# Expert chosen from 8 tiles instead of 16, its first rows gathered in the scatters' queue, and half of the first block's product moved into the last two attention rounds

## The chip, the cores and the metric

The kernel runs on one core of a Trainium2 chip. A core has five engines with a queue of instructions each: TensorE (matmuls and transposes, PE in the profile, its weight loads PEld), VectorE (DVE), ScalarE (ACT), GpSimd (POOL) and SyncE (SP, which here only issues transfers). Transfers run on 16 DMA engines. The metric is the device time of one execution in microseconds; the median of the runs counts.

## The reference

Three parts, one behind the other, on 3072 rows of 384 numbers:

```python
for t in range(S):                                   # 1: attention with a decaying state, 4 x 8 heads of 48
    cur = np.einsum('bhd,bhe->bhde', u[None] * kt, vt)
    y[:, :, t] = np.einsum('bhd,bhde->bhe', rt, state + cur)
    state = wt[:, :, :, None] * state + np.einsum('bhd,bhe->bhde', kt, vt)

logits = x @ w_gate + modality_bias[modality_id]     # 2: one of 8 experts for each row
e_idx = np.argmax(logits, axis=1)
h = np.maximum(x[mask] @ w1[e], 0.0)                 #    F = 1024
out[mask] = gate_w[mask, None] * (h @ w2[e])

h = np.maximum(np.maximum(x @ w1, x @ w2), x @ w3)   # 3: a network of width 768
return (h @ w_out)
```

## The kernel before

**Attention** runs in 24 rounds, one for each tile of 128 rows (L895 on, `for i in range(NTILE)`). The rounds overlap: round i computes the scans of tile i+2 (`scan_f`, L745, at its start, and `scan_r`, L761), the scores of tile i+1 (`scores`), and the output of tile i (`output`, TensorE, L805 and L811). VectorE turns the output into x one round later (`output_x`, L830), so output(22) is TensorE's work in round 22 and x(22) is VectorE's at the start of round 23; x(i) goes to DRAM (`xs`). In each round GpSimd masks the scores of tile i+1 (`am`, L781), makes the u-term of tile i+2 (L708, L709), and scales v by its sum (L718), which x needs. SP issues the loads of tile i+3 (`nat`, `vt`) and of tile i+5 (`tq`), a round or so before they are used; ScalarE checks the w columns of tile i+4 as they come (`flags`, L723).

**Routing** goes in batches of tiles, 8, 8, 3, 2 and 3. Behind a batch's last tile `route_batch` is put in a list, and `slot()`, which is called some six times a round, runs a few steps of it: about 16 small VectorE instructions, two small TensorE matmuls, and at the end one scatter for each tile (`scatter`, L297, an indirect transfer issued by GpSimd). A scatter writes the row numbers of a tile, sorted by expert, into a DRAM list (`order`). `do_scatters` issues them one at a time, at two places of a round.

**Choosing.** Behind the second batch (`NG` = 16 tiles) `choose_first` takes the expert that has the most rows so far (13 small VectorE instructions, and a flag `few` if it has fewer than 512). `first_load` loads that expert's weights in seven pieces (w1 three, w2 four). `settle` is a GpSimd memset of the places that the scatters have read, so it waits until they have landed; behind it `first_ids` gathers row numbers from `order`, and `first_rows` gathers the rows of the first two blocks from `xs`. `split_w1` and `split_w2` cut the weights into a high part (ScalarE's copy, `w1h`) and a low part (`w1l`, `w2l`, L500, VectorE or GpSimd), since each product is made of three matmuls in a reduced format.

**The first network** goes over 13 blocks of 256 rows: blocks 0 and 1 of the chosen expert, an extra block X with that expert's remaining rows, and ten more. `x_part` turns the gathered rows into columns (`xh`, `xl`: TensorE transposes, L1129); `g1` is the first product in four quarters of 18 matmuls, `g2` the second. The last batch's routing and the plan of the blocks (the generator `chain`, which `go(n)` runs n steps of) lie within block 0. **The second network** follows over six pairs of blocks.

What lies where around the end of attention is written out by hand: a table of hooks, {(round, place): functions}, the counts in `FIRST_GO` for `go`, and the counts of dummy matmuls in `WARM`. The code's order is each engine's order.

Of the kernel before, what the change touches and what calls it, by code (L numbers as in the profile page):

```python
# [33 lines left out]
W2_FIRST = range(8)  # L34
RATE = (2, 6, 4)
# [6 lines left out]
FIRST_GO = (2, 2, 4, 0, 0, 2, 4, 4, 0, 0, 6)  # L42
WARM = (16, 6, 4, 0, 3, 6, 6, 3, 3)
# [3 lines left out]
def kernel(ctx: ExitStack, tc: tile.TileContext, rkw_t, v_t, vrk, u, modality, w_gate, bias, w1, w2, v1, v2,  # L47
# [17 lines left out]

    TW = 256
    EARLY = 2
    NG = -(-E * TW // 128)

    batches = [(t, 8) for t in range(0, NG, 8)]  # L70
    for n in (3, 2, 3):
        batches.append((sum(batches[-1]), n))
    assert NG % 8 == 0 and sum(batches[-1]) == NTILE
# [12 lines left out]
    def mmt():  # L86
        return pools["mm"].tile([128, 512], F32, tag="mm", name="mm")
# [152 lines left out]

    scatters = []

    def route_batch(batch, then=(), lead=0):
# [20 lines left out]
        for _ in range(lead and GAP[0]):  # L264
            yield SLOT
# [34 lines left out]
        scatters.extend([lambda c=c: scatter(c) for c in range(nb)])  # L300

# [9 lines left out]
    def do_scatters(n=NTILE):  # L311
        if scatters and "filled" in carry:
            carry.pop("filled")()
        for sc in scatters[:n]:
            sc()
        carry["scattered"] = carry.get("scattered", 0) + len(scatters[:n])
        del scatters[:n]
# [275 lines left out]
    def attention(hooks):  # L593
        with ExitStack() as es:
# [242 lines left out]
            rate = [1]  # L837
# [21 lines left out]
            carry["warm"] = warm  # L859
            loads, rows = constants_rest(pes)  # L860
# [34 lines left out]
            for i in range(NTILE):  # L895
# [31 lines left out]
                if i < NTILE - 3:  # L927
                    do_scatters(1)
# [11 lines left out]
                slot()  # L940
                if i:
                    warm(WARM[5] if i == NTILE - 1 else WARM[6] if i == NTILE - 2 else WARM[4 if i % NC == NC - 1 else 3])
                    T[i - 1].clear()
                if i < NTILE - 3:
                    do_scatters(1)
# [3 lines left out]
                if i and i == t0 + nb:  # L949
                    later.append(route_batch((t0, nb), (choose_first,) if i == NG else (), LEAD))  # L950
                    rate[0] = RATE[(i == NG) + 2 * (i > NG)]
# [5 lines left out]
            while later:  # L957
                run(later.pop(0))
# [80 lines left out]
    class Experts:  # L1039
# [74 lines left out]
        def room(self, s, eng=POOL):  # L1114
            s["xin"] = [self.px.tile([128, DM], F32, tag="xin", name="xin") for _ in range(2)]
            for xin in s["xin"]:
                eng.memset(xin, 0.0)
# [173 lines left out]
    def first_rows(j):  # L1291
        for half in range(2):
            ex.gather(T[j], half, NG * 128)

    def first_x():
        for half in range(2):
            go(FIRST_GO[half])
            ex.x_part(T[0], half)
            carry["warm"](WARM[7 + half])
        go(FIRST_GO[2])  # L1300

# [30 lines left out]
    def first_block(vw):  # L1332
# [6 lines left out]
        for s, cur in enumerate(seq):  # L1339
            nx = seq[s + 1] if s <= N - 1 else None  # L1340
            for q in range(4):
                if s == 0:
                    ex.g1((q,), lambda: go(FIRST_GO[2 * q + 3]))
# [5 lines left out]
                elif s < EARLY:  # L1349
                    if s == 0:  # L1350
                        ex.split_w2((2 * q, 2 * q + 1), W2_FIRST)
                        go(FIRST_GO[2 * q + 4])
# [62 lines left out]
    def rest():  # L1415
# [3 lines left out]
        with tc.If(lastv > 0):  # L1419
# [7 lines left out]
            with ExitStack() as es:  # L1427
# [14 lines left out]
                with tc.If(fewv > 0):  # L1442
                    for j in range(1, EARLY):
# [9 lines left out]
    with tc.manual_schedule():  # L1453
# [4 lines left out]
        def ex_room(j, eng):  # L1458
            ex.room(T[j], eng)
        attention({(NG + 3, "mid"): [chosen, bind(first_load, 0, 0)],  # L1460
                   (NG + 3, "end"): [bind(first_load, 0, 1)],
                   (NG + 4, "mid"): [bind(first_load, 0, 2)],
                   (NG + 4, "end"): [bind(first_load, 1, 0)],
                   (NG + 5, "mid"): [bind(first_load, 1, 1)],
                   (NG + 5, "end"): [bind(first_load, 1, 2), bind(ex.open_rows, wes)],
# [71 lines left out]
```

## Time and profile before

| | |
|---|---|
| median of 3 runs | 784.94 us (784.89 to 790.58) |
| the profiled execution | 783.83 us, of which the span from first to last instruction is 781.7 |
| attention, routing | to about 222 us |
| first network | about 222 to 500 us |
| second network | to the end |
| busy shares of the span | PE 92%, PEld 83%, DVE 67%, POOL 46%, ACT 40% |

A row of the timeline gives start, duration, engine, line, operation, `out<-in`, the number of merged instructions, and in brackets the idle time of the engine before it with what ended it. The rows below all come from the profiled execution.

### The profile page before, as it was taken

What the parts mean: (1) busy time and instruction counts of PE and PEld (TensorE: products, weight loads), DVE (VectorE), ACT (ScalarE), POOL (GpSimd) and SP (SyncE); (2) the same over time, 40 slices, a digit from 0 to 9 for tenths busy, and PEclk for the clock granted to TensorE, in tenths of its full rate; (3) what the DMA queues carried; (4) which work ended last, traced back from release to release, by engine and by line L of the source; (5) the groups of instructions that cost most, each with busy time, mean ns of one, the idle gap of its engine ahead of it and who ended that gap; (6) DMA issues with size and microseconds to landing.
All of it is one profiled execution on the core that took longest, in us unless ns stands there. A gap on an engine that the chain in (4) does not pass through costs nothing.

```text
span 781.7 us, 13036 instructions
## 1 busy us (share of the span) xinstructions
PE 718.9 (92%) x4745; PEld 649.5 (83%) x4746; DVE 519.9 (67%) x975; ACT 313.9 (40%) x705; POOL 362.8 (46%) x389
## 2 busy tenths in 40 slices
PE   6889887887699999999999999999999999999991
PEld 3778787777589989999999998798988989889891
DVE  5999999999668798878897889624224243242320
ACT  5556545444241465566666653221212222112210
POOL 7698769858676477766665354120100201002000
PEclk9799989979789999999999999999999999999996
DMA  9878879968412322222226134020100200001000
GB/s 243 201 203 244 225 178 187 205 176 217 81 52 90 93 71 63 80 80 66 63 73 223 41 125 158 1 82 0 68 15 0 82 1 21 20 1 41 0 17 29
DMA packets 32382, 74.57 MB, mean 95 GB/s; under 512 B 5973, under 2 KB 19061, under 8 KB 32308
## 3 DMA queue, kind: packets, MB, share of 16 engines
q1 hardware_dynamic: 27508, 64.15, 30.5%
q0 software_dynamic: 4800, 9.49, 3.8%
q8 instruction: 39, 0.64, 0.4%
q14 instruction: 35, 0.29, 0.1%
HBM read 87.96 MB, written 14.38 MB: 131 GB/s over the span
## 4 chain that ended last, share of the span: by engine, by line
issue 39%; DVE 23%; PE 21%; POOL 7%; DMA 5%; ACT 1%; SPq 1%; POOLq 0%; DVEq 0%; ACTq 0%
PE mm L1142 7%; PE mm L1141 6%; PE mm L1140 6%; DVE prod L745 3%; DVE prod L761 3%; POOL out_dram L1225 3%; DMA tq<-in_rkw_t_dram 3%; DVE w1l L500 2%; POOL w2l L500 1%; DVE rt L754 1%; DVE tq L730 1%; DVE sh L714 1%; DVE x L830 1%; DMA w2r<-in_moe_w_dram 1%; DVE kvb L818 1%
## 5 line engine op out<-in xcount | busy, mean ns | idle before, releaser
L1205 DVE TENSOR_TENSOR w2r<-mm,w2r 128x512 f32<-128x512 f32 x72 | 49.7, 690 | 146.9 <-PE mm L1142 146.8
L1225 POOL DMA_INDIRECT out_dram<-w2r,oi_all x24 | 25.9, 1078 | 247.2 <-ACT w2r L1224 246.5
L1140 PE MATMUL mm<-w1h,vh 128*128 128x512 f32 x324 | 127.7, 394 | 1.3 <-DVE w2r L1205 1.3
L1142 PE MATMUL mm<-w1h,vl 128*128 128x512 f32 x324 | 127.1, 392 | 0.0
L1141 PE MATMUL mm<-w1l,vh 128*128 128x512 f32 x324 | 125.9, 389 | 0.0
L1142 PE MATMUL mm<-xh,w1l 128*128 128x256 f32 x312 | 89.4, 287 | 3.0 <-DVE w1l L500 3.0
L1142 PE MATMUL mm<-hh,w2l 128*128 128x256 f32 x312 | 89.1, 286 | 1.0 <-POOL w2l L500 0.8
L1141 PE MATMUL mm<-hl,w2h 128*128 128x256 f32 x312 | 88.5, 284 | 1.0 <-DVE hl L1154 1.0
L1140 PE MATMUL mm<-hh,w2h 128*128 128x256 f32 x312 | 89.2, 286 | 0.0
L1140 PE MATMUL mm<-xh,w1h 128*128 128x256 f32 x312 | 88.5, 284 | 0.0
L1141 PE MATMUL mm<-xl,w1h 128*128 128x256 f32 x312 | 88.3, 283 | 0.2 <-DVE xl L1134 0.2
L1207 ACT CAST w2h<-w2r 128x512 fp32r<-128x512 f32 x36 | 22.3, 621 | 136.7 <-DVE w2r L1205 136.6
L1140 PEld LDWEIGHTS mm<-w1h,vh 128*128 128x128 f32 x324 | 60.9, 188 | 14.0 <-DVE w2r L1205 2.0
L1142 PEld LDWEIGHTS mm<-w1h,vl 128*128 128x128 f32 x324 | 60.8, 188 | 14.0
L1141 PEld LDWEIGHTS mm<-w1l,vh 128*128 128x128 f32 x324 | 60.8, 188 | 13.3
L500 DVE TENSOR_TENSOR w1l<-w1r,w1h 128x512 fp32r<-128x512 f32 x66 | 51.6, 835 | 24.3 <-ACT w1h L498 24.2
L500 POOL TENSOR_TENSOR w2l<-w2r,w2h 128x384 fp32r<-128x384 f32 x40 | 46.2, 1160 | 40.2 <-ACT w2h L498 38.4
L805 PE MATMUL yb<-nat,am 128*128 128x56 f32 x384 | 53.0, 297 | 12.3 <-DVE lh L832 9.7
L1142 PEld LDWEIGHTS mm<-xh,w1l 128*128 128x128 f32 x312 | 59.8, 192 | 5.1 <-DVE w1l L500 5.1
L805 PEld LDWEIGHTS yb<-nat,am 128*128 128x128 f32 x384 | 50.7, 213 | 14.3 <-POOL am L781 5.3
L1142 PEld LDWEIGHTS mm<-hh,w2l 128*128 128x128 f32 x312 | 59.7, 191 | 2.6 <-POOL w2l L500 1.2
L1141 PEld LDWEIGHTS mm<-hl,w2h 128*128 128x128 f32 x312 | 59.7, 191 | 1.5 <-DVE hl L1154 1.4
(244 smaller groups left out, 1757.2 us busy)
## 6 DMA issues: line engine op xcount, KB each, us to landing
w1r<-in_moe_w_dram SPq DMA_DIRECT2D x10, 1536.0 KB, 7.1
w2r<-in_moe_w_dram SPq DMA_DIRECT2D x10, 1536.0 KB
nat<-in_vrk_dram SPq DMA_DIRECT2D x24, 608.0 KB, 6.9
tq<-in_rkw_t_dram SPq DMA_DIRECT2D x46, 288.0 KB, 6.8
stg<-in_moe_w_dram SPq DMA_DIRECT2D x18, 384.0 KB, 3.1
vt<-in_v_t_dram SPq DMA_DIRECT2D x24, 192.0 KB, 7.0
x2t<-raw SPq DMA_DIRECT2D x12, 384.0 KB, 2.4
w1r<-x2t SPq DMA_DIRECT2D x12, 384.0 KB, 3.8
```

Of the source, the lines that this page charges most:

```text
L500: eng.tensor_tensor(out=lo, in0=src, in1=hi.bitcast(F32), op=ALU.subtract)
L714: DVE.tensor_reduce(out=s["sh"], in_=heads(s["k"]), axis=AX.X, op=ALU.add)
L730: DVE.tensor_scalar(out=wr, in0=wr, scalar1=W_LO, scalar2=W_HI, op0=ALU.max, op1=ALU.min)
L745: DVE.tensor_tensor_scan(out=prod, data0=f[:, 1023:1535], data1=d1f, initial=0.0, op0=ALU.mult, op1=ALU.add)
L761: DVE.tensor_tensor_scan(out=prod[:, 0:511][:, ::-1], data0=f[:, 1025:1536][:, ::-1], data1=d1r[:, 0:511][:, ::-1], initial=0.0, op0=ALU.m ...
L805: PE.matmul(yb[:, h * DV:(h + 1) * DV], lhsT=s["am"][:, 4 * (h % 2) + h // 2, :], rhs=s["v"][:, h, :], start=(h == 0), stop=(first and h = ...
L1140: PE.matmul(oc, lhsT=wh[:, kk, sl], rhs=xh[:, kk, :], start=first and kk == 0, stop=False)
L1141: PE.matmul(oc, lhsT=wh[:, kk, sl], rhs=xl[:, kk, :], start=False, stop=False)
L1142: PE.matmul(oc, lhsT=wl[:, kk, sl], rhs=xh[:, kk, :], start=False, stop=last and kk == nk - 1)
L1205: DVE.tensor_tensor(out=hv, in0=o, in1=hv, op=ALU.max)
L1207: ACT.copy(self.h2h[:, c, :], hv)
L1225: ins = POOL.indirect_dma_start(out=out[:, :], out_offset=bass.IndirectOffsetOnAxis(ap=ids[q][:, 0:1], axis=0), in_=ob, in_offset=None, bo ...
```

## The change

- The batches become 8, 8, 5 and 3, and `NG` becomes 8: the expert is chosen from the first 8 tiles. Its weights are loaded in rounds 13 to 19, one piece a round, instead of rounds 19 to 22.
- `settle` and the eight gathers (four of ids, four of rows) go into the list of scatters, behind the first batch's eight and two empty entries; `do_scatters` issues them two a round like scatters. The row tiles are filled with zeros by ScalarE in round 14 instead of by GpSimd.
- Block 0's columns and the first three `split_w1` come in round 22 behind the scores, the first quarter of `g1` in round 23, the second quarter behind the last round, and the rest of the routing within it. Products during attention use the small pool `tp`.
- Four of the eight low parts of w2 are made by GpSimd instead of VectorE, two and two in round 23.
- The dummy matmuls of the last two rounds and those around block 0's columns are gone (6 + 6 + 3 + 3).

```diff
-W2_FIRST = range(8)
-RATE = (2, 6, 4)
+W2_FIRST = range(4, 8)
+RATE = 4
-FIRST_GO = (2, 2, 4, 0, 0, 2, 4, 4, 0, 0, 6)
-WARM = (16, 6, 4, 0, 3, 6, 6, 3, 3)
+FIRST_GO = (8, 1, 7, 2, 6)
+WARM = (16, 6, 4, 0, 3)
...
-    NG = -(-E * TW // 128)
...
+    batches = [(0, 8), (8, 8), (16, 5), (21, 3)]
+    NG = sum(batches[0])
...
+        if sum(batch) == NG and lead:
+            scatters.extend([lambda: None] * 2 + [lambda: settle(0, NG)] + first_gathers)
...
-                if i < NTILE - 3:
-                    do_scatters(1)
+                do_scatters(2 if i >= NTILE - 2 else 1)
...
-    def first_ids(j):
-        do_scatters(max(0, NG - carry["scattered"]))
-        if j == 0:
-            settle(0, NG)
-        for q in (2 * j, 2 * j + 1):
-            ex.gather_ids(oi_all[:, q, :], idxg[:, q:q + 1])
+    def first_ids(q):
+        ex.gather_ids(oi_all[:, q, :], idxg[:, q:q + 1])
+
+    def first_room():
+        ex.open_rows(wes)
+        for j in range(EARLY):
+            ex.room(T[j], carry["zero"])
...
+    def first_rows(q):
+        ex.gather(T[q // 2], q % 2, NG * 128)
+    first_gathers.extend([lambda q=q: first_ids(q) for q in range(2 * EARLY)])
+    first_gathers.extend([lambda q=q: first_rows(q) for q in range(2 * EARLY)])
...
-                   (e - 3, "uterm"): [bind(first_ids, 0)],
-                   (e - 2, "start"): [bind(ex.split_w1, (0, 1, 2))],
-                   (e - 2, "uterm"): [bind(ex_room, 0, POOL), bind(first_rows, 0)],
...
-                   (e - 2, "end"): [bind(first_ids, 1), bind(ex.split_w1, (3, 4, 5), "h")],
-                   (e - 1, "mid"): [bind(ex.split_w1, (3, 4, 5), "l"), bind(ex_room, 1, POOL), bind(first_rows, 1)],
...
-                   (e, "mid"): [first_x, bind(ex.split_w2, (0, 1), W2_FIRST, "h")],
+        hooks = {(13, "mid"): [chosen, bind(first_load, 0, 0)],
+                 (14, "end"): [first_room],
+                 (e - 2, "uterm"): [first_x, bind(ex.split_w1, (0, 1, 2))],
+                 (e - 2, "late"): [bind(ex.split_w1, (3, 4, 5), "h")],
+                 (e - 1, "uterm"): [bind(ex.split_w1, (3, 4, 5), "l"), bind(ex.g1, (0,)),
+                                    bind(ex.split_w2, (0, 1), W2_FIRST)],
+                 (e - 1, "mid"): [bind(ex.split_w2, (2, 3), W2_FIRST)],
+                 (e, "mid"): [bind(ex.g1, (1,), rest_of_routing)],
+                 (e, "end"): [bind(ex.split_w2, (4, 5), W2_FIRST)]}
+        for q in range(1, 7):
+            hooks[(13 + q, "mid")] = [bind(first_load, q // 3 if q < 6 else 1, q if q < 3 else q - 3)]
```

On GpSimd's queue in rounds 21 and 22 the kernel before has, in a row, three scatters, the memset of `settle`, two gathers of ids, and only then the scaling of v (`nat<-nat,sh`) and the masking of the scores (`am`):

```order
L708 TENSOR_TENSOR nat<-nat,u_b 128x384
L709 TENSOR_TENSOR nat<-nat 128x384
L297 DMA order<-idg,places 24576x2 x3
L309 MEMSET places 128x16
L1110 DMA oi_all<-order,idxg 128x2 x2
L718 TENSOR_TENSOR nat<-nat,sh 128x448
L781 AFFINE_SELECT am<-am 128x512 x2
L1117 MEMSET xin 128x384 x2
L1121 DMA xin<-xs,oi_all 128x384 x2
```

The kernel after has the memset and the gathers in rounds 16 to 20, one at a time (the first of them here; lines are three to seven further on):

```order
L721 TENSOR_TENSOR nat<-nat,sh 128x448
L784 AFFINE_SELECT am<-am 128x512 x2
L711 TENSOR_TENSOR nat<-nat,u_b 128x384
L712 TENSOR_TENSOR nat<-nat 128x384
L313 MEMSET places 128x8
L721 TENSOR_TENSOR nat<-nat,sh 128x448
L1117 DMA oi_all<-order,idxg 128x2
L784 AFFINE_SELECT am<-am 128x512 x2
L711 TENSOR_TENSOR nat<-nat,u_b 128x384
L712 TENSOR_TENSOR nat<-nat 128x384
L1117 DMA oi_all<-order,idxg 128x2
```

So the memset and all eight gathers leave the stretch in which L718 and `am` of the last tiles are made.

On TensorE the kernel after has, in rounds 22 and 23, the transposes of block 0's rows (`tp<-ident,xin`) between the scores and gate(23), and the first quarter of the product (`tp<-xh,w1h` and its two fellows, 18 rows, of which two stand here) behind output(22) and a routing matmul:

```order
L780 MATMUL mm<-rt,kt 128x128 x8
L1136 MATMUL tp<-ident,xin 128x128 x6
L705 MATMUL tp<-wgb,vt 128x64 x3
L808 MATMUL yb<-nat,am 128x56 x8
L814 MATMUL yb<-sbd_149,rt 128x112 x4
L269 LDWEIGHTS sut_bf
L269 MATMUL lgps<-oh,sut_bf 128x40
L270 LDWEIGHTS ones_bf
L270 MATMUL lgps<-ohx,ones_bf 128x40
L1147 MATMUL tp<-xh,w1h 128x256
L1148 MATMUL tp<-xl,w1h 128x256
```

Before, these transposes and the whole first product stand behind output(23), its routing matmul and dummies.

On SP's queue the kernel after has, in rounds 13 and 14, a piece of w1 between the loads of one round and those of the next; before, the first of these pieces stands behind the loads of round 19:

```order
L677 DMA tq_162<-in_rkw_t_dram 48x1536 x2
L1282 TENSOR_LOAD gctl
L1282 ISA x2
L1288 ISA
L1288 DMA w1r<-in_moe_w_dram 128x1024
L836 DMA xs<-x 128x384
L682 DMA nat<-in_vrk_dram 128x1216
L687 DMA vt<-in_v_t_dram 128x384
L677 DMA tq_163<-in_rkw_t_dram 48x1536 x2
L1288 ISA
L1288 DMA w1r<-in_moe_w_dram 128x1024
```

The queue itself is in order, so in rounds 13 to 19 a weight piece now goes out ahead of the next round's `nat`, `vt` and `tq`.

## Rows read from the trace of the kernel before

**Rows 1.** Stretches: busy us and instructions of each engine, PE clock, DMA share, GB/s.
```profile
116.00:145.00 29.00, 22.88 (x194) 20.59 (x194) 28.66 (x48) 13.76 (x41) 27.48 (x26) 0.94 0.98 192
145.00:163.00 18.00, 15.12 (x123) 13.60 (x125) 17.62 (x37) 9.40 (x28) 11.53 (x13) 0.88 0.97 229
163.00:176.00 13.00, 12.25 (x80) 10.71 (x79) 12.45 (x41) 5.53 (x17) 8.46 (x7) 0.64 0.49 128
...
213.00:219.00 6.00, 6.00 (x27) 4.89 (x27) 2.71 (x12) 0.00 (x0) 5.11 (x5) 0.50 0.25 70
222.40:241.20 18.80, 18.60 (x156) 18.31 (x156) 16.43 (x63) 7.85 (x18) 10.30 (x11) 1.00 0.07 15
...
320.00:340.00 20.00, 19.73 (x159) 18.98 (x158) 17.69 (x27) 12.34 (x27) 13.25 (x14) 1.00 0.22 74
420.00:440.00 20.00, 19.98 (x168) 19.77 (x166) 15.21 (x26) 13.10 (x29) 10.65 (x12) 1.00 0.55 184
```

**Rows 2.** Timeline of VectorE: the first scan of rounds 15 to 19.
```profile
136.84 1.21 DVE L745 TENSOR_TENSOR_SCAN prod<-tq,d1f 128x512 f32<-128x512 f32 x1
...
145.17 1.22 DVE L745 TENSOR_TENSOR_SCAN prod<-tq,d1f 128x512 f32<-128x512 f32 x1
...
152.38 1.58 DVE L745 TENSOR_TENSOR_SCAN prod<-tq,d1f 128x512 f32<-128x512 f32 x1
...
162.77 1.22 DVE L745 TENSOR_TENSOR_SCAN prod<-tq,d1f 128x512 f32<-128x512 f32 x1
...
173.08 1.22 DVE L745 TENSOR_TENSOR_SCAN prod<-tq,d1f 128x512 f32<-128x512 f32 x1
```

**Rows 3.** Timeline of all engines, rounds 22 and 23: x(21), the memset, x(22), output(23).
```profile
200.53 0.55 DVE L830 TENSOR_TENSOR x<-yb,nat 128x384 f32<-128x384 f32 x1
...
206.95 0.11 POOL L309 MEMSET places<- 128x16 int32 x1 [5.43 <-DMA order<-idg,places]
...
211.09 0.56 DVE L830 TENSOR_TENSOR x<-yb,nat 128x384 f32<-128x384 f32 x1 [6.36 <-POOL nat L718]
...
212.04 3.63 PE L805 MATMUL yb<-nat,am 128*128 128x56 f32 x16 [4.83 <-DVE lh L832]
```

**Rows 4.** Timeline of TensorE: the transposes for block 1 and for X.
```profile
231.75 0.82 PE L1129 MATMUL tp<-ident,xin 128*128 128x128 f32 x6
...
255.56 0.82 PE L1129 MATMUL tp<-ident,xin 128*128 128x128 f32 x6
```

**Rows 5.** Timeline of all engines: durations of steps that are moved or moved past.
```profile
194.49 1.94 PE L805 MATMUL yb<-nat,am 128*128 128x56 f32 x16
...
196.27 1.10 PE L811 MATMUL yb<-sbd,rt 128*128 128x112 f32 x8
...
198.66 1.95 DVE L500 TENSOR_TENSOR w1l<-w1r,w1h 128x512 fp32r<-128x512 f32 x3
...
199.49 1.07 ACT L780 COPY am<-mm 128x512 f32<-128x512 f32 x2 [2.73 <-PE mm L777]
...
220.60 0.48 ACT L1133 CAST xh<-tp 128x384 fp32r<-128x384 f32 x1 [15.54 <-PE tp L1129]
...
221.11 0.56 DVE L1134 TENSOR_TENSOR xl<-tp,xh 128x384 fp32r<-128x384 f32 x1 [1.21 <-ACT xh L1133]
```

**Rows 6.** The page's costliest groups: busy us, mean ns of one, idle before.
```profile
L500 POOL TENSOR_TENSOR w2l<-w2r,w2h 128x384 fp32r<-128x384 f32 x40 | 46.2, 1160 | 40.2 <-ACT w2h L498 38.4
```

**Rows 7.** DMA issues from 90 to 235 us: count, KB each, median us to landing.
```profile
w1r<-in_moe_w_dram SPq DMA_DIRECT2D x3, 512.0 KB
w2r<-in_moe_w_dram SPq DMA_DIRECT2D x4, 384.0 KB, 8.9
```

**Rows 8.** Timeline of ScalarE, round 16: the check of w columns.
```profile
154.00 0.72 ACT L723 ACTIVATE jk<-tq,neglo 128x512 bf16<-128x512 f32 x1 [3.10 <-DMA tq<-in_rkw_t_dram]
```

**Rows 9.** Timeline of GpSimd: the last scatters' memset, and the second gather of X's rows.
```profile
238.68 0.10 POOL L309 MEMSET places<- 128x8 int32 x1 [3.69 <-DMA order<-idg,places]
...
244.19 1.00 POOL L1121 DMA_INDIRECT xin<-xs,oe  x1 [0.31 <-issue]
```

More of the change, by code (lines that the diff above doesn't have):

```diff
@@ L67 @@
     EARLY = 2
-    NG = -(-E * TW // 128)
[L70 to L73, printed above, removed]
+    batches = [(0, 8), (8, 8), (16, 5), (21, 3)]
+    assert all(a + n == b for (a, n), (b, _) in zip(batches, batches[1:])) and sum(batches[-1]) == NTILE
+    NG = sum(batches[0])
     batch_of = {t: b for b in batches for t in range(b[0], b[0] + b[1])}
@@ L241 @@
     scatters = []
+    first_gathers = []
     def route_batch(batch, then=(), lead=0):
@@ L263, in route_batch @@
         carry["t"] = ohx[:, :, nb]
-        for _ in range(lead and GAP[0]):
+        for _ in range(lead and GAP[0] if t0 < NTILE - 8 else 1):
             yield SLOT
@@ L836, in attention @@
             later = []
-            rate = [1]
+            rate = [2]
             def slot():
@@ L859, in attention, with run_later @@
             carry["warm"] = warm
+            def run_later():
+                while later:
+                    run(later.pop(0))
+                do_scatters()
+            carry["later"] = run_later
+            carry["zero"] = lambda t: ACT.copy(t, wide[:, 0:DM])
             loads, rows = constants_rest(pes)
@@ L949, in attention @@
                 if i and i == t0 + nb:
-                    later.append(route_batch((t0, nb), (choose_first,) if i == NG else (), LEAD))
-                    rate[0] = RATE[(i == NG) + 2 * (i > NG)]
+                    later.append(route_batch((t0, nb), (choose_first,) if i == NG else (), LEAD if i < NTILE - 3 else 1))
+                    rate[0] = RATE
                 if i == 0:
@@ L1282, in first_load, with rest_of_routing @@
                      .rearrange("a (k p) f -> p (a k) f", p=128))
-    def first_ids(j):
-        do_scatters(max(0, NG - carry["scattered"]))
-        if j == 0:
-            settle(0, NG)
-        for q in (2 * j, 2 * j + 1):
-            ex.gather_ids(oi_all[:, q, :], idxg[:, q:q + 1])
-    def first_rows(j):
-        for half in range(2):
-            ex.gather(T[j], half, NG * 128)
+    def first_ids(q):
[8 more added lines that the diff above has]
+    first_gathers.extend([lambda q=q: first_rows(q) for q in range(2 * EARLY)])
     def first_x():
         for half in range(2):
-            go(FIRST_GO[half])
             ex.x_part(T[0], half)
-            carry["warm"](WARM[7 + half])
-        go(FIRST_GO[2])
+    def rest_of_routing():
+        carry["later"]()
+        go(FIRST_GO[0])
     def bind(f, *a):
@@ L1442, in rest @@
                 with tc.If(fewv > 0):
-                    for j in range(1, EARLY):
+                    for j in range(EARLY):
                         one(j, SP.value_load(ctl[0:1, 2 * j:2 * j + 1], min_val=0, max_val=E - 1))
```

36 lines of the change are left out of this document (13 added, 23 removed).

## The prediction

> **What bounds the kernel now.** I read the stages first [rows 1]. From 222.4 us on TensorE is full (18.60 of 18.80 us) at a clock of 1.00, and it stays so through both networks; the change does not touch that work, which only starts earlier or later. Before that the attention loop is paced by VectorE (28.66 of 29 us in 116 to 145, 17.62 of 18 in 145 to 163), while the DMA engines are all but full (0.98 and 0.97). A round's length is the distance of its first scan (L745) to that of the next [rows 2]: 8.33 us for round 15, with two scatters from GpSimd in it, 7.21 for round 16 with none, 10.39 and 10.31 for rounds 17 and 18, with 9 and 20 small routing instructions.
>
> The hand-over lies between the two stages [rows 3]. In round 21 GpSimd's memset L309 (the kernel's `settle`) stands for 5.43 us, until 206.95, for a scatter to land. Behind it in GpSimd's order come two gathers of ids and then L718, for which VectorE's x(22) waits 6.36 us; TensorE starts output(23) only at 212.04. After x(23) come the columns of the first block, and at 222.4 its first matmul. That block's first product has four quarters of 18 matmuls. 156 matmuls start in 18.8 us [rows 1], 0.12 us each, and the transposes that follow the fourth quarter start at 231.75 [rows 4], so the second quarter starts at 231.75 - 54 x 0.12 = 225.2. This is the point that I follow, because in the new order, too, the second quarter is the first to come behind output(23).
>
> **The change part by part.** All of it against the profiled execution (span 781.7, its time 783.83).
>
> (a) To x(21), which is at 200.53 [rows 3]. One of the short batches falls away: 9 + 3 + 4 = 16 small VectorE instructions in rounds 20 and 21. Round 18, with 20 of them, lasts 3.10 us longer than round 16, 0.155 each; round 17, with nine, 3.18 longer, 0.35 each [rows 2]. So 2.5 to 5.6 us less; I take 2.5, from the round that has more of them. The 13 instructions that choose the expert go from round 18 to round 10, the same price both ways, 0. The three `w1l` (1.95 us [rows 5]) move behind x(21): 1.95 less here, counted again in (b). The eight gathers come up into rounds 16 to 20, where GpSimd issued five scatters and will issue eight gathers and one scatter, four more. A pair costs its round 8.33 - 7.21 = 1.1 us: 2.2 for four, 5.0 if all nine counted, nothing where GpSimd idles (it was busy 11.53 of 18 us in 145 to 163 [rows 1]). I take 1.5, between the half-idle stretch and the full pairs. The memset comes a round and a half behind the last of its scatters, over 10 us, against the 5.43 that it waited: 0. ScalarE fills the four row tiles in round 14, about half a microsecond each by its copies [rows 5]; VectorE paces that round, so 0, and 2 if ScalarE were late there. Together -2.5 - 1.95 + 1.5 = -2.95: x(21) at 197.6.
>
> (b) From x(21) to the second quarter. ScalarE's copies of am end at 200.56 here [rows 5]; the round's front shifts by -2.5 + 1.5 = -1.0, so at 199.6, 2.0 behind x(21). Then xh (0.48) and xl (0.56): 3.0. gate(23) is estimated at 0.7, a quarter of output's matmuls, and output(22) takes 2.9, as output(21) from 194.49 to 197.37 [rows 5]: done at 6.6. VectorE meanwhile: x and logits until 1.0, xl 3.0, w1l 5.0, five routing instructions 5.8, the state's two 7.0, four more 7.6, a sum 8.2, three more 8.7; x(22) and lh until 9.5. The routing's matmul L269 stands in TensorE's order ahead of the first quarter and needs the 7.6. So: first quarter 7.9 to 10.1, output(23) until 13.0, then the second quarter, 197.6 + 13.0 = 210.6, which is 14.6 us before 225.2. The second three w1l and the first quarter's hl (2.0 + 0.6) lie under output(23). Four of the eight w2l go from VectorE to GpSimd and are needed by the second product, three quarters (6.5 us) later; if that cover is gone each costs up to 1.16 us [rows 6].
>
> (c) The seven weight loads, 512 KB three times and 384 KB four times [rows 7], go from rounds 19 to 22, where the loop has few loads left, into rounds 13 to 19, each behind that round's loads and ahead of the next round's in SP's queue. In 116 to 145 192 GB/s were moved at a share of 0.98, in 145 to 163 229 at 0.97 [rows 1]: 512 KB take 2.7 or 2.3 us that were not free. ScalarE already waits 3.10 us for w columns in round 16 [rows 8], and nobody pays, since VectorE is full. The three loads of w1 are 8.2 us of new lateness at the slower rate; from 163 to 176 the share is only 0.49, so some 6.6 us come free again. I take half of the 8.2, 4.0 us on the path; bounds 0 (all behind VectorE) and 8.2. The Trainium skill (DMA: Bandwidth & Descriptors, Issuing engines are not separate DMA queues) says that transfers issued by any engine run on the same 16 DMA engines and interleave; by that, gathers in the scatters' queue win no transfer time, and the full 8.2 would be paid wherever those engines are full.
>
> (d) The 18 dummy matmuls of rounds 22 and 23 and behind them are gone. Behind 4.83 us of idling, output(23) ran at the lower of the clock's two levels (0.50 from 213 to 219 [rows 1]); its larger part took 3.63 us [rows 3] instead of 1.94 [rows 5]. That long idling goes, but short ones stay in round 22. Either nothing is lost, or output(22), the quarter and output(23) all run at half speed: 2.9 + 2.2 + 2.9 = 8.0. I take 2.0, nearest to one of the three. The Trainium skill (TensorE: Matmul & The Clock Gate, Part 1) says that the clock falls to half behind idle time and comes back under load; by it the dummies were worth keeping, and the 8.0 would be paid.
>
> (e) The extra block X needs the last tiles' ids. Its rows are issued by 245.19 [rows 9] and TensorE turns them at 255.56 [rows 4], about 10 us of room. TensorE comes some 8 us earlier after (c) and (d), while GpSimd reaches that point with four w2l and seven scatters in its queue. If its chain came no earlier at all, 2 us of room would be left; if (c) and (d) cost nothing, 4.3 would be missing. I take 0.5; bounds 0 and 4.3.
>
> Sum: -14.6 + 4.0 + 2.0 + 0.5 = -8.1, and 783.83 - 8.1 = 775.7. The median of the runs, 784.94, is 1.1 above the profiled one: **776.8**.
>
> **The rivals.** First, all is hidden: (c), (d) and (e) cost nothing. 784.94 - 14.6 = 770.3. For it: VectorE is full anyway, 3.10 us of waiting passed unseen, and the DMA engines are half idle behind 163. Against it: some 12 us of transfers are pressed into a stretch at 0.97.
>
> Second, the other side: the weight loads land on the path one by one. Place: SP's queue in rounds 13 to 19, where the loop's own loads, issued a round ahead, stand behind them. Price: three times 2.7 plus four times 1.7 (384 KB at 229 GB/s) = 15.0; with (d) and (e) 17.5 against 14.6, so 787.8. It decides once the loop's loads come later than the roughly 3 us that ScalarE now waits unseen.
>
> Third, the change does not do what it says: the first 1024 rows hold fewer than 512 of the chosen expert, the flag `few` is set, and blocks 0 and 1 are done over at the end, by themselves. At least the first network's 18.8 us each, 37.6, so over 807. Against it: weights are loaded again only where the expert changes, and traffic rises only at 420 to 440 (184 GB/s against 74 in 320 to 340 [rows 1]), so one expert has about ten of twelve blocks, some 850 of 1024 rows.
>
> **How the numbers follow.** Forecast (gain 5 to 12 us) 0.50, all hidden 0.20, loads on the path 0.22, blocks done over 0.03, something else 0.05. The range goes from the first rival's 770.3, with 2 us for (a), to the second's 787.8 less 1: 768 to 787. A difference of 1%, 7.8 us, is about what a measurement here can tell from none; the forecast lies on that line, so half of its chance goes either way. With the first rival and most of the unnamed, faster 0.49; within 1% 0.42; slower 0.09 (a tail of the second rival, the third, some unnamed).
>
> **What the changed profile would show.** (a) Round 10 near 10 us, round 18 near 8, and no GpSimd memset that waits over 1 us in the loop. (b) output(23) directly behind the first quarter, the second quarter near 216, with (c) and (d) in it. (c) ScalarE's waits for w columns in rounds 14 to 18: far above 3 us if the loads are on the path, none above 3 if they are hidden. (d) The clock in the last two rounds, 1.00 or 0.50. (e) TensorE's transposes for X waiting for a gather or not. I am wrong above all if the loop up to round 21 is much longer than now, or if both networks no longer take the same time from the second quarter to the end.

## The result, and the profile after

The changed kernel takes 781.1 us (median of 13 runs, 778.13 to 783.90), the kernel before 788.78 (13 runs, 784.89 to 790.58). The ratio is 0.9917, with a 95% interval of 0.9900 to 0.9934: 0.8% faster, some 6.5 us. The profiled execution took 778.13 us with a span of 776.3, against 783.83 and 781.7. The prediction said 776.8, between 768 and 787; the time lies inside, and within 1% of before, to which the prediction had given 0.42 and to faster 0.49. It started from 784.94, the median of three runs, where thirteen give 788.78, so 3.8 of the 4.3 us between 776.8 and 781.1 lie in that starting point. The gain, 8.1 us forecast and some 6.5 measured, was near in part only because errors of both signs met in its sum.

The scans of the attention rounds on VectorE (start, duration), to be held against [rows 2] and against x(21) and x(22) in [rows 3]; the timeline of the changed kernel:

```profile
165.99 1.22 DVE L748 TENSOR_TENSOR_SCAN prod<-tq,d1f 128x512 f32<-128x512 f32 x1
...
174.31 1.22 DVE L748 TENSOR_TENSOR_SCAN prod<-tq,d1f 128x512 f32<-128x512 f32 x1
...
181.34 1.58 DVE L748 TENSOR_TENSOR_SCAN prod<-tq,d1f 128x512 f32<-128x512 f32 x1
...
188.95 1.21 DVE L748 TENSOR_TENSOR_SCAN prod<-tq,d1f 128x512 f32<-128x512 f32 x1
...
196.45 0.55 DVE L833 TENSOR_TENSOR x<-yb,nat 128x384 f32<-128x384 f32 x1
199.96 1.02 DVE L1141 TENSOR_TENSOR xl<-tp,xh 128x384 fp32r<-128x384 f32 x2 [2.53 <-ACT xh L1140]
200.98 3.29 DVE L503 TENSOR_TENSOR w1l<-w1r,w1h 128x512 fp32r<-128x512 f32 x3
...
206.70 0.29 DVE L236 TENSOR_TENSOR oh<-req,ram 128x40 bf16<-128x40 f32 x1
...
208.19 0.56 DVE L833 TENSOR_TENSOR x<-yb,nat 128x384 f32<-128x384 f32 x1
```

Round 18 lasts 8.32 us (10.31 before), round 20 lasts 7.61 (10.69 before). x(21) stands at 196.45, 4.1 us earlier; x(22) at 208.19, 2.9 earlier, and it waits for nothing. Of the 4.1 us, 0.8 are there at the start of round 7 already (72.23 against 73.02), a time that differs by more than that between profiles of the changed kernel's code (see below).

TensorE around the hand-over, the changed kernel:

```profile
207.05 0.19 PE L269 MATMUL lgps<-oh,sut_bf 128*128 128x40 bf16 x1 [0.61 <-DVE oh L236]
...
207.44 0.55 PE L1147 MATMUL tp<-xh,w1h 128*128 128x256 f32 x1
...
211.42 2.07 PE L808 MATMUL yb<-nat,am 128*128 128x56 f32 x16
...
214.20 0.36 PE L1147 MATMUL tp<-xh,w1h 128*128 128x256 f32 x1
...
219.69 0.18 PE L269 MATMUL lgps<-oh,sut_bf 128*128 128x24 bf16 x1 [0.95 <-DVE oh L236]
...
222.24 0.82 PE L1136 MATMUL tp<-ident,xin 128*128 128x128 f32 x6
...
246.55 0.82 PE L1136 MATMUL tp<-ident,xin 128*128 128x128 f32 x6
```

The first quarter starts at 207.44, output(23) follows directly behind it, and the second quarter starts at 214.20, 11.0 us ahead of the prediction's 225.2. But of these 11.0 only 9.5 are left at the transposes of block 1 (222.24 against 231.75), 9.0 at those of X (246.55 against 255.56, [rows 4]), and 5.4 at the end. Where the last 3.0 go is seen in the second network. GpSimd issues a scatter of output rows at the end of each of its blocks; the changed kernel's (start, duration, wait):

```profile
503.86 1.97 POOL L1232 DMA_INDIRECT out_dram<-w2r,oi_all  x1 [17.75 <-ACT w2r L1231]
...
550.88 1.38 POOL L1232 DMA_INDIRECT out_dram<-w2r,oi_all  x1 [39.94 <-ACT w2r L1231]
...
601.15 1.39 POOL L1232 DMA_INDIRECT out_dram<-w2r,oi_all  x1 [39.94 <-ACT w2r L1231]
...
751.97 0.97 POOL L1232 DMA_INDIRECT out_dram<-w2r,oi_all  x1 [39.94 <-ACT w2r L1231]
```

And the same places in the kernel before:

```profile
512.20 1.97 POOL L1225 DMA_INDIRECT out_dram<-w2r,oi_all  x1 [17.51 <-ACT w2r L1224]
...
558.65 1.35 POOL L1225 DMA_INDIRECT out_dram<-w2r,oi_all  x1 [39.28 <-ACT w2r L1224]
...
608.32 1.36 POOL L1225 DMA_INDIRECT out_dram<-w2r,oi_all  x1 [39.28 <-ACT w2r L1224]
...
757.32 0.97 POOL L1225 DMA_INDIRECT out_dram<-w2r,oi_all  x1 [39.27 <-ACT w2r L1224]
```

A block lasts 50.27 us after and 49.66 before, on a TensorE that is busy all of the time at a granted clock of 1.00 in both. The lead falls from 8.3 to 5.4 us over five blocks of code that the change does not touch.

### The profile page after: what moved, and what is told of

Read it like the earlier page. It is cut to its first block, busy times and chain, and to the rows that moved or that the text cites. A ratio compares the mean times of both kernels' runs of the same rounds, so it can differ in the third digit from the quotient of the medians.

```text
span 776.3 us, 12971 instructions
## 1 busy us (share of the span) xinstructions
PE 723.7 (93%) x4725; PEld 652.2 (84%) x4726; DVE 519.7 (67%) x953; ACT 313.6 (40%) x706; POOL 365.7 (47%) x389
## 4 chain that ended last, share of the span: by engine, by line
issue 41%; DVE 22%; PE 22%; POOL 8%; DMA 3%; ACT 2%; POOLq 0%; SPq 0%; ACTq 0%; DVEq 0%
PE mm L1149 6%; PE mm L1147 5%; PE mm L1148 5%; POOL out_dram L1232 3%; DVE prod L748 2%; DVE w1l L503 2%; DVE prod L764 2%; DMA vt<-in_v_t_dram 2%; DVE rt L757 1%; POOL w2l L503 1%; DVE tq L733 1%; DVE sh L717 1%; PE yb L808 1%; DMA w2r<-in_moe_w_dram 1%; PE kvb L801 1%
## 5 line engine op out<-in xcount | busy, mean ns | idle before, releaser
L1148 PE MATMUL mm<-w1l,vh 128*128 128x512 f32 x324 | 128.1, 395 | 0.0
L1149 PE MATMUL mm<-xh,w1l 128*128 128x256 f32 x300 | 85.9, 286 | 2.4 <-DVE w1l L503 2.4
L1147 PE MATMUL mm<-xh,w1h 128*128 128x256 f32 x300 | 85.0, 283 | 0.0
L1148 PE MATMUL mm<-xl,w1h 128*128 128x256 f32 x300 | 84.8, 283 | 0.0
L1214 ACT CAST w2h<-w2r 128x512 fp32r<-128x512 f32 x36 | 22.3, 621 | 139.4 <-DVE w2r L1212 139.4
L503 POOL TENSOR_TENSOR w2l<-w2r,w2h 128x384 fp32r<-128x384 f32 x44 | 49.8, 1139 | 42.1 <-ACT w2h L501 40.3
L1149 PEld LDWEIGHTS mm<-xh,w1l 128*128 128x128 f32 x300 | 57.5, 192 | 4.4 <-DVE w1l L503 4.4
L1147 PEld LDWEIGHTS mm<-hh,w2h 128*128 128x128 f32 x312 | 59.8, 192 | 0.0
L1147 PEld LDWEIGHTS mm<-xh,w1h 128*128 128x128 f32 x300 | 57.6, 192 | 0.0
```

What stands on the lines that cost most here:

```text
L503: eng.tensor_tensor(out=lo, in0=src, in1=hi.bitcast(F32), op=ALU.subtract)
L1147: PE.matmul(oc, lhsT=wh[:, kk, sl], rhs=xh[:, kk, :], start=first and kk == 0, stop=False)
L1148: PE.matmul(oc, lhsT=wh[:, kk, sl], rhs=xl[:, kk, :], start=False, stop=False)
L1149: PE.matmul(oc, lhsT=wl[:, kk, sl], rhs=xh[:, kk, :], start=False, stop=last and kk == nk - 1)
L1214: ACT.copy(self.h2h[:, c, :], hv)
```

## The experiments

All ratios are to the kernel before, timed on the same chip; the changed kernel's own is 0.9917. The start of round 7 differs between executions, from 72.2 to 75.7 us in the profiles of the changed kernel and its variants, by waits in the loop's first rounds that no edit reaches. Positions behind it are therefore given from x(21) on: in the changed kernel the second quarter comes 17.75 us behind x(21) (214.20 - 196.45), the end of the span 579.9. What the expectations call the scan of tile 21, at 196.45, is this x(21). The stretch from the second quarter to the first scatter of the second network varies too: 288.6 to 291.1 us in the six profiles that have the changed kernel's code there (its own has 289.7), so that differences of 1 or 2 us at the end of a single span show nothing by themselves.

**The place of the second network's weight tiles.** The two kernels put `vh`, `vl`, `voh` and `vol` at different bytes of a partition: among the mask tiles of the routing scans (`d0c`) the one for 2 tiles (96 bytes) gives way to one for 5 (192 bytes), which moves them from byte 24736 to 24832; it is not one mask tile more, as the expectation has it. The first run moves them alone:

```
         wres = pool(ctx, "wres", 1)
+        wres.tile([128, 40], F32, name="spare")
```

> The changed kernel with 160 spare bytes ahead of the eight second network's weight tiles, so that the first of them stands at byte 24992 of a partition instead of 24832; nothing else differs. The product loop of the second network, compared between the two profiles, runs at 233.3 ns from one 128x512 product to the next after the change and at 228.8 ns before, and one of its five blocks takes 50.27 us against 49.66 us: 3.0 us of the gain are lost there, in a part that the change does not touch except that one more mask tile of the scans moved these tiles from byte 24736 to byte 24832. Theory (the place of the tiles sets the pace): a block takes 49.7 us again and the median is near 778, 3 us under the changed kernel's 781.1. Rival (the pace belongs to the chip or the execution, or to the order of the code): the block takes 50.3 us here and the median stays within 1 us of 781.1.

Measured: median 776.11, ratio 0.9859 (0.9824 to 0.9894), 4.6 us below the changed kernel by the ratios. Its profile has x(21) at 196.44 and the second quarter at 214.11, as before the edit, but shorter blocks:

```profile
598.63 1.38 POOL L1232 DMA_INDIRECT out_dram<-w2r,oi_all  x1 [39.23 <-ACT w2r L1231]
...
648.19 1.38 POOL L1232 DMA_INDIRECT out_dram<-w2r,oi_all  x1 [39.23 <-ACT w2r L1231]
...
697.76 1.39 POOL L1232 DMA_INDIRECT out_dram<-w2r,oi_all  x1 [39.23 <-ACT w2r L1231]
```

A block takes 49.57 us, 0.7 less, 3.5 in five blocks. The other 1.1 us lie in the first network (the first scatter of the second comes at 502.73 instead of 503.86), no more than two profiles of one code differ there. The other way round, in the kernel before, whose tiles go to byte 24832:

```
+    ct([128, 24], F32, "spare")
```

> The kernel before with 96 spare bytes among its small constants, so that the second network's weight tiles stand at byte 24832 as in the changed kernel, and every tile of the attention stage 96 bytes higher too. Theory (place of the tiles): a block of the second network takes 50.27 us instead of 49.66 us, and the kernel is 3 us slower than the kernel before in the paired runs. Rival (pace of the execution, or of the changed code): 49.7 us, within 1 us of the kernel before.

Measured: 790.39, ratio 1.0043 (1.0019 to 1.0067), blocks of 50.27 us, the changed kernel's figure to the hundredth. So the place sets the pace of a block, in both kernels. Which property of it? In these products `w1h` and `w1l` (w1h at byte 157664) stream against weights loaded from `vh` and `vl`. Three more runs: 32 spare bytes between each two of the six tiles; the expert's tiles 64 bytes down (`p.tile([128, 16], F32, name="spare")` behind `hl`); and 64 spare bytes ahead of `vh`.

> The changed kernel with 32 spare bytes between each two of the second network's six weight tiles, so that the first halves stand 0, 32 and 64 bytes and the second halves 96, 128 and 160 bytes beyond the places of the changed kernel (byte 24832 and 9216 bytes further each). Each run of nine products reads one pair of them, so that one profile shows three pairs of places. Theory (what matters is whether a tile starts on a multiple of 64 bytes, as at 24832 and unlike 24736 and 24992): products that load their weights from tiles at 0, 64 and 128 stand 233.3 ns apart and those from tiles at 32, 96 and 160 stand 228.5 ns apart. Rival (coarser steps matter, 128 or 256 bytes): 64, or 64 and 128, are like 32.

> The changed kernel with 64 spare bytes that move the weight and row tiles of the expert's network, w1h and w1l among them, 64 bytes down, from byte 157664 to 157600 and so on; the second network's tiles, which TensorE loads as weights, stay at 24832. In the second network's loop w1h and w1l are what streams against those weights. Theory (the pace comes from where the loaded weights stand): a block of the second network takes 50.27 us as in the changed kernel; the expert's products, 0.12 us apart, keep their pace or change it by up to 2%, up to 4 us either way. Rival (the pace comes from the place of the one relative to the other): a block of the second network changes from 50.27 us, to 49.6 or to more.

> The changed kernel with 64 spare bytes ahead of the second network's weight tiles, which then stand at byte 24896, a multiple of 64 and of 128 as 24832 is, but not of 256. Blocks of that network took 50.27 us at 24832, 49.66 at 24736 and 49.57 at 24992 (the latter two are 32 beyond a multiple of 64 and 160 beyond one of 256). Theory (a multiple of 64 is the slow place): 50.3 us, median within 1.5 us of the changed kernel's 781.1. Rival (a coarser step of 256 bytes decides, and 24832 is slow for being a multiple of it): a block takes 49.6 to 49.9 us, median 2 to 4 us lower. The run with 32 bytes between the tiles (49.99 us a block) has not told these apart.

| vh at | w1h at | w1h - vh | block, us | product to product, ns | kernels |
|---|---|---|---|---|---|
| 24736 | 157664 | 132928 = 2077 x 64 | 49.66 | 229.0 | before |
| 24992 | 157664 | 132672 = 2073 x 64 | 49.57 | 228.9 | changed with 160 bytes, two more |
| 24832 | 157664 | 132832 = 2075.5 x 64 | 50.27 | 233.3 | changed, before with 96 bytes, five more |
| 24896 | 157664 | 132768 = 2074.5 x 64 | 50.67 | 234.3 | changed with 64 bytes |
| 24832 | 157600 | 132768 = 2074.5 x 64 | 50.67 | 234.3 | changed, expert's tiles 64 down |

The last column but one is the mean of the 805 steps from one product to the next in the traced blocks. The last two rows have different tiles moved, the same distance, and the same pace to 0.01 us a block: in these runs it is the distance of the streamed tile from the loaded one that counts, not the place of either, and the multiple of 64 or 256 for the loaded tile alone falls as a theory. The four distances fit a rule that multiples of 64 bytes are fast; the run with 32 bytes between the tiles (49.99 us a block, 231.5 ns on average, 232.2, 231.9 and 230.6 ns for its three pairs of tiles, 779.3 us in its one run) bore out neither its theory nor its rival and did not sort its products by that rule pair by pair, so the rule stays open. The 64-byte runs took 782.63 (ratio 0.9930, 0.9906 to 0.9955) and 782.51 (0.9932, 0.9905 to 0.9959). The expert's products of 256 columns stand 119.9 to 120.0 ns apart in all fourteen profiles; but their two tiles always moved together, so their distance was never changed, and whether it matters there is not known.

**The dropped batch.** The changed kernel with `(16, 3), (19, 2)` in place of `(16, 5)`:

```
-    batches = [(0, 8), (8, 8), (16, 5), (21, 3)]
+    batches = [(0, 8), (8, 8), (16, 3), (19, 2), (21, 3)]
```

> The changed kernel with the routing batches of before, (16,3) and (19,2) in place of (16,5), and 96 spare bytes so that no other tile moves. Theory (the batch that was dropped took 2.5 us off the last rounds): the scan of tile 21 starts 2.5 us later than the 196.45 us of the changed kernel and the second quarter of the first product at 216.7 instead of 214.2; median 2 to 3 us above the changed kernel. Rival (the batch's VectorE work fitted in gaps, and the rounds are set by the loads): tile 21 within 0.7 us, median within 1 us.

Measured: 785.42, ratio 0.9972 (0.9944 to 1.0000), 4.3 us above the changed kernel. Round 20 takes 11.21 us instead of 7.61, and round 21 is 3.4 longer, with a wait that the changed kernel has not:

```profile
207.04 0.56 DVE L834 TENSOR_TENSOR x<-yb,nat 128x384 f32<-128x384 f32 x1 [3.26 <-POOL nat L722]
```

So x(21) comes 7.0 us later, not 2.5; behind it 2.9 are won back, since the second quarter follows 14.9 us behind x(21) instead of 17.75.

The opposite, the kernel before with the joined batch alone (and its tiles at 24992):

```
-    for n in (3, 2, 3):
+    for n in (5, 3):
```

> The kernel before with the routing batches (16,3) and (19,2) joined to (16,5), as the changed kernel has it, and nothing else of the change; the second network's weight tiles are put at byte 24992, where a block of that network took 49.57 us, so that their place costs nothing. Theory (the dropped batch carries a large part of the gain: the changed kernel lost 4.3 us of median when the batch was put back): the second quarter, at 225.2 before, starts 2.5 to 4.5 us earlier, and the kernel is 2.5 to 4.5 us faster than the kernel before. Rival (the batch only hurts where the first tile's columns stand in the same rounds): within 1 us of the kernel before.

Measured: 786.03, ratio 0.9970 (0.9951 to 0.9990), 2.4 us below the kernel before, 0.5 of them from blocks of 49.57 us. Its round 20 takes 7.66 us, 3.0 less, yet its second quarter starts at 224.88, only 0.2 earlier than that of the kernel before (the row itself stands at 225.11), or 0.9 counted from the start of round 7: GpSimd's memset waits for the scatters until 206.59 all the same (206.95 in [rows 3]), and x(22) waits 6.53 us for what stands behind it. In this profile little of the 3 us comes through while GpSimd waits for the scatters; the medians show about 1.9 us, and that difference is not explained. The measured 2.4 us lie between the theory (2.5 to 4.5) and the rival (within 1).

**The weight loads back in rounds 19 to 22.**

```
-        hooks = {(13, "mid"): [chosen, bind(first_load, 0, 0)],
+        hooks = {(13, "mid"): [chosen],
...
-        for q in range(1, 7):
-            hooks[(13 + q, "mid")] = [bind(first_load, ...)]
+        for q in range(7):
+            hooks[(19 + q // 2, "end" if q % 2 else "mid")] = [bind(first_load, ...)]
```

> The changed kernel with the seven loads of the expert's weights issued in rounds 19 to 22, as in the kernel before, instead of 13 to 19. Theory of the prediction (its term of +4.0 us for loads that take the place of the tiles' own loads in rounds 13 to 19): the scan of tile 21 starts up to 4 us earlier than at 196.45, the median falls by 2 to 4 us. Theory after the result (the traced rounds 13 to 19 are only 0.7 us longer in sum with the loads in them, so they ride along there): nothing is gained, and rounds 20 to 22, where the loads now stand, grow; median 0 to 3 us above the changed kernel's 781.1.

Measured: 780.20, ratio 0.9905 (0.9875 to 0.9934), not to be told from the changed kernel. Rounds 12 to 15 last 8.09, 8.31, 9.28 and 8.35 us without the loads and 8.08, 8.32, 9.28 and 8.35 with them; rounds 13 to 18 together 51.8 without and 51.4 with. The loads cost nothing that can be seen in either place.

**Dummies back in the last two rounds** (6 in each):

```
-                    warm(WARM[4 if i % NC == NC - 1 else 3] if i < NTILE - 2 else 0)
+                    warm(WARM[4 if i % NC == NC - 1 else 3] if i < NTILE - 2 else 6)
```

> The changed kernel with six dummy products in each of the last two rounds, where it has none. Theory (the fall of the granted clock to 0.50 from 204 to 211 us follows from a TensorE with little to do, and costs 1.9 us in the first quarter and 1.5 us in the output ahead of it): the clock stays higher there, the first quarter's 18 products stand 0.12 us apart instead of 0.21, the second quarter starts 2 to 3 us earlier than 214.2, and the median falls by as much. Rival (the dummies stand in the queue ahead of the output and the quarter, and the wait that ends last is VectorE's or GpSimd's): the clock is higher but the second quarter is within 0.7 us of 214.2, or later; median within 1 us or up to 2 us higher.

Measured: 781.54, ratio 0.9925 (0.9895 to 0.9954). Output(22) runs at the full clock, and TensorE then waits longer for the same VectorE instruction (TensorE's timeline of this kernel):

```profile
204.60 1.10 PE L814 MATMUL yb<-sbd,rt 128*128 128x112 f32 x8
208.57 0.18 PE L269 MATMUL lgps<-oh,sut_bf 128*128 128x40 bf16 x1 [2.87 <-DVE oh L236]
```

That row is 10.6 us behind x(21) (197.98), exactly as in the changed kernel (207.05 - 196.45). So output(22) at the half clock was off the path; VectorE sets this point. Behind the 2.87 us of idling the clock falls all the same, to 0.50 from 210 to 212; two thirds of the quarter run slowly, and the second quarter comes 19.7 us behind x(21), 1.9 later than in the changed kernel: the dummies themselves stand ahead of the first quarter for 1.5 us and ahead of the second for 1.1. What a first quarter at the full clock alone would give was not measured.

**The first quarter behind output(23).**

```
-    (e - 1, "uterm"): [..., bind(ex.g1, (0,)), ...]
-    (e, "mid"): [bind(ex.g1, (1,), rest_of_routing)]
+    (e - 1, "uterm"): [...]
+    (e, "mid"): [bind(ex.g1, (0,)), bind(ex.g1, (1,), rest_of_routing)]
```

> The changed kernel with the first quarter of the first product issued after the last tile's output instead of ahead of it. Theory (it runs in a wait of TensorE for the last tile's scan, so that it costs nothing there and its own length behind it): the second quarter starts 2.2 us later (18 products of 0.12 us at the full clock) to 3.9 us later (at the half clock), and the median rises by as much. Rival (it is hidden either way, because the next wait, for the last batch's VectorE work, ends at the same time): the first block's ends are within 0.7 us and the median within 1 us of the changed kernel.

Measured: 781.48, ratio 0.9917 (0.9891 to 0.9943). The second quarter comes 20.9 us behind x(21), 3.1 later; at the transposes of block 1 that is 1.7, because the wait of 0.95 us for the last batch's `oh` (219.69 above) is gone from it, at those of X 1.2 and at the end of the span 0.8. The median is the rival's, the 1.7 us at the first block's end are not. By the two intervals the medians can hide some 2.4 us either way, so all that is shown is that the 2.2 to 3.9 us of the theory are not paid in full.

**Columns and both quarters behind output(23).** As the last, with `first_x` moved from (e - 2, "uterm") to the head of (e, "mid").

> The changed kernel with the first tile's columns (their transposes, casts and remainders) and both quarters of its product issued behind the last tile's output; the early gathers, the splits of the weights and the batches stay as changed. Theory (the hand-over waits that went with the early gathers are one part of the gain, and the columns and the half product inside the last rounds another): VectorE's round for tile 22 loses a wait of 2.5 us and 1.0 us of remainders, so tile 22's output comes some 3 us earlier, and then transposes, casts and the first quarter follow one by one; the second quarter starts near 217 instead of 214.2, and the median rises by 2 to 4 us. Rival (what stands in the last rounds costs VectorE there as much as it saves behind them): the second quarter is within 1 us of 214.2, median within 1 us.

Measured: 783.88, ratio 0.9958 (0.9937 to 0.9979), 3.2 us above the changed kernel by the ratios. TensorE's chain is then the one that was expected, one step behind the other:

```profile
211.12 3.63 PE L808 MATMUL yb<-nat,am 128*128 128x56 f32 x16 [1.75 <-DVE logits L837]
...
216.35 1.49 PE L1136 MATMUL tp<-ident,xin 128*128 128x128 f32 x6
...
218.45 0.36 PE L1147 MATMUL tp<-xh,w1h 128*128 128x256 f32 x1 [0.61 <-ACT xh L1140]
```

Against the prediction's point in the kernel before, 24.7 us behind its x(21) (225.2 - 200.53), the second quarter comes 22.3 behind here (20.5 were expected) and 17.75 in the changed kernel.

**A version that goes on from there.** In round 22 VectorE idles 2.53 us for ScalarE's casts and has three `w1l` behind the wait. They go ahead of it, their ScalarE half earlier still, with the 160 spare bytes:

```
-    (e - 2, "uterm"): [first_x, bind(ex.split_w1, (0, 1, 2))],
+    (e - 3, "late"): [bind(ex.split_w1, (0, 1, 2), "h")],
+    (e - 2, "uterm"): [bind(ex.split_w1, (0, 1, 2), "l"), first_x],
```

> The changed kernel with the first three splits of the first weights ahead of the first tile's columns instead of behind them, their ScalarE half one round earlier, and the second network's weight tiles at byte 24992 as in the run with 160 spare bytes (776.1 us). Theory (VectorE sets the length of these rounds: in round 22 it waits 2.5 us for ScalarE's casts of the columns, and the three remainders of 3.3 us behind that wait can fill it): from the scan of tile 21 to the routing product takes 8 us instead of 10.6, the second quarter starts 2 to 2.5 us earlier, the median falls to 773.5 to 774.5. Rival (TensorE at the half clock, whose gate product now waits longer for the remainders, or the last batch's VectorE work, ends last): the second quarter is within 0.7 us of where it was, median within 1 us of 776.1.

Measured: 775.93, ratio 0.9855 (0.9828 to 0.9883), the same as with the spare bytes alone. The second quarter does come 15.6 us behind x(21), 2.1 earlier, the transposes of block 1 1.8 earlier and those of X 1.7; 0.7 us of that are left at the end of the span. Behind X's transposes the two profiles differ by 0.9 us, which profiles of one code do as well, so whether the 2 us were lost or are hidden by the spread of the runs (the two intervals allow some 3.5 us either way) stays open. Both versions are faster than either kernel, by 1.4% against the one before.

## Why the prediction was right, and where it was not

The direction, the point that moves and the range held; the terms of the sum did not all. By the rows the hand-over is shorter because nothing waits on GpSimd for a scatter any more, and its announced signs are there: round 10 at 10.75 us, round 18 at 8.32, no memset of GpSimd that waits in the loop, output(23) directly behind the first quarter, the second quarter at 214.2 for "near 216". The terms one by one, in the profiled executions:

- (a) x(21) came 4.1 us earlier for 2.95, or 3.3 counted from the start of round 7. The batch gave 3.1 in round 20 for 2.5. The choice of the expert was an even trade, as said: +0.8, +3.3 and -1.4 in rounds 9 to 11, -0.5 and -2.0 in 17 and 18. The three `w1l` gave 2.4 in round 21 for 1.95. Rounds 7 and 14 lost 0.9 each. VectorE is busy for 10.34 of round 10's 10.75 us with 34 instructions; it paces these rounds. The gathers, priced at 1.5, cost little: rounds 16 and 19 are 0.1 and 0.2 longer. Their price was a misreading. The pair of scatters in round 15 of the kernel before is not what costs 1.1 us. All of VectorE's instructions in rounds 15 and 16 last the same, but for the scan L761, beside which GpSimd's L718 runs in the one round and not in the other (timeline of the kernel before, all engines):

```profile
139.74 2.34 DVE L761 TENSOR_TENSOR_SCAN prod<-tq,d1r 128x511 f32<-128x511 f32 x1
...
140.03 0.95 POOL L718 TENSOR_TENSOR nat<-nat,sh 128x448 f32<-128x448 f32 x1
...
147.13 0.93 POOL L718 TENSOR_TENSOR nat<-nat,sh 128x448 f32<-128x448 f32 x1
...
148.07 1.22 DVE L761 TENSOR_TENSOR_SCAN prod<-tq,d1r 128x511 f32<-128x511 f32 x1
```

  So a scatter or gather costs by where GpSimd's next tensor instruction comes to stand. The 0.9 us of round 14 are of this kind: its first scan takes 2.14 us instead of 1.22, with L711 beside it. No run isolates this.
- (c) The loads' 4.0 us are the term that failed: 0 by the run with the loads moved back. ScalarE's wait for w columns, the announced sign, was never above 3:

```profile
132.39 0.72 ACT L726 ACTIVATE jk<-tq,neglo 128x512 bf16<-128x512 f32 x1 [2.69 <-DMA tq<-in_rkw_t_dram]
```

  The step that was wrong is that a DMA share of 0.97 meant full. The windows of [rows 1], in the changed kernel:

```profile
116.00:145.00 29.00, 26.49 (x209) 23.60 (x207) 28.06 (x49) 15.49 (x45) 27.15 (x26) 0.82 0.98 218
145.00:163.00 18.00, 15.48 (x132) 14.14 (x132) 17.72 (x35) 9.44 (x29) 17.29 (x17) 0.93 1.03 260
163.00:176.00 13.00, 11.09 (x75) 8.73 (x75) 12.55 (x32) 5.54 (x18) 10.84 (x10) 0.76 0.96 250
```

  At shares that are hardly higher they move 218 and 260 GB/s instead of 192 and 229. Like for like, in the run with the loads moved back, the 29 us that answer to the first of these stretches have a share of 0.93 at 182 GB/s, and the rounds are as long. The page that the prediction named for this term (the Trainium skill, DMA: Bandwidth & Descriptors, Issuing engines are not separate DMA queues) would have all transfers share the 16 engines; that may be, but here they had room, and the full 8.2 us that the prediction drew from it were not paid.
- (b) and (d), from x(21) to the second quarter: 17.75 us for 13.0 + 2.0. The largest part is VectorE: `oh`, whose routing matmul stands ahead of the first quarter, was expected 7.6 us behind x(21) and is done at 10.5. `xl` was counted with one half (0.56; both take 1.02), it starts 1.0 us later, and the three `w1l` behind it take 3.29 us instead of 1.95. Beside them GpSimd makes the masks, which take 2.02 us instead of 1.23; beside the three of 1.95 in the kernel before, and beside the next three here, it only issues scatters (GpSimd's and VectorE's timelines of the changed kernel):

```profile
201.70 2.02 POOL L784 TENSOR_SCALAR_AFFINE_SELECT am<-am 128x512 f32<-128x512 f32 x2
...
209.10 1.93 DVE L503 TENSOR_TENSOR w1l<-w1r,w1h 128x512 fp32r<-128x512 f32 x3
```

  In the last version above, with GpSimd's L712 beside the second of them, they take 2.69. The clock costs what was taken: 0.50 from 202 to 211, and 18 products in 4.0 us instead of 2.2; output(22), slow as well, is hidden, as the run with dummies shows. The Trainium skill's rule (TensorE: Matmul & The Clock Gate, Part 1) that the clock halves behind idling agrees with these rows; that the dummies were worth keeping does not follow from it: with them the time is the same.
- (e) X came in time: no transpose waits for it. What took its place was the last batch, which VectorE now reaches so late that TensorE waits for its `oh` within the first block (219.69): from the third quarter to the fourth 3.6 us pass instead of 2.2, 1.3 more. Another 0.5 us are lost to X's transposes and 0.7 from there to the second network, the latter within what profiles of one code differ by.
- The sum's silent premise, that both networks take the same time from the second quarter to the end, is what the prediction named as its way to be wrong "above all", and it was: 562.1 us for 556.5. Of the 5.6, 3.0 are the place of the tiles and 1.3 the last batch. With the tiles at 24992 the span is 771.8, 9.9 below before.

Of the rivals, "all is hidden" was right in its mechanism for the loads and for X and wrong for the clock (1.8 us); its 770.3 also lacks VectorE's extra 2.8 us, the last batch and the place of the tiles. "The loads land on the path" is excluded by the run that moves them.

As to the parts of the change, each known to 2 or 3 us only: the batch is worth 4.3 us where the hand-over's waits are gone and about 2 us where they are not; columns and quarters together 3.2; the early first quarter by itself and the early loads nothing that the runs can tell. The gathers in the scatters' queue, with which the wait for the scatters went, were not undone alone, nor were the changed rate of the routing steps (`RATE`) and the share of `w2l` that went to GpSimd; that the shorter hand-over comes from the gathers rests on the rows of the two kernels, and is not shown by a run.

## What to carry to other kernels

A part that the change does not touch can still change: a mask tile that grew by 96 bytes moved the weight tiles of a network that runs hundreds of microseconds later, and took back a third of the gain, so compare the profile beyond the changed stage, block by block. A high busy share of the DMA engines is no rate; what is late is told by who waits. And on an engine that is full, price a moved step by its instructions there, whole, look at what other engines do beside them, and look at what the freed engine then waits for: each wait that went here uncovered another, shorter one.

## What the hardware showed that was not expected

- TensorE's pace in the second network followed the distance in SBUF between the streamed and the loaded tile: 229.0, 233.3 or 234.3 ns from one 128x512 product to the next, at a granted clock of 1.00 each time, which is 3.0 us of this network's 250 between the two kernels.
- The same share of busy DMA engines, 0.97 to 1.03, stood beside 192 to 260 GB/s.
- VectorE's scan took longer where GpSimd was computing: in the kernel before, the first scan of a tile lasts 1.20 to 1.23 us the 12 times that no TENSOR_TENSOR of GpSimd is running at its start, and 1.29 to 2.04 us the 12 times that one is.
- Executions that run the same code differ by up to 3.5 us within the loop's first eight rounds, by up to 1.6 us in a few single rounds behind them, and by up to 2.5 us in the first network.
